# A convolution by short transforms: how the kernel weights are loaded and spread at the start

## The chip, the cores and the metric

The kernel runs on one core of a Trainium2 chip. The core has five engines that run side by side and meet only at semaphores: TensorE (matrix products into PSUM, an accumulator memory of eight banks), VectorE, ScalarE and GpSimd (elementwise work; only the first two of these read PSUM here), and SyncE, which issues transfers between the chip's main memory and the on-chip memory SBUF (128 partitions). The metric is the device time of one execution in microseconds; lower is better. In the profile TensorE appears as PE (the products) and PEld (the loading of the stationary operand), VectorE as DVE, ScalarE as ACT, GpSimd as POOL, SyncE's transfer issues as SPq.

## The reference

An image of 224 x 224 pixels with 96 channels is convolved, around its edges, with a 7 x 7 kernel from 96 to 96 channels, by way of the Fourier transform:

```python
B, H, W, C = x.shape          # 1, 224, 224, 96
K = w.shape[0]                # 7
wp = pad(w, ((0, H - K), (0, W - K), (0, 0), (0, 0)))
Xf = rfft2(x.astype(float32), axes=(1, 2))
Wf = rfft2(wp.astype(float32), axes=(0, 1))
Yf = einsum('bhwi,hwio->bhwo', Xf, Wf)
y = irfft2(Yf, s=(H, W), axes=(1, 2)).astype(bfloat16)
```

Inputs and outputs are bfloat16. Since the kernel is only 7 rows and columns, the same result can be had by short transforms over blocks.

## The kernel before, in words

Rows are cut into eight blocks of 28 (`NJ`, `B`), each transformed over 34 rows (`L`), which gives 17 frequencies (`NS`). Columns are not transformed; along them the seven taps are applied directly, with three products saved by sums and differences of taps and of even and odd columns (`TAPS`, ten tap combinations per frequency, `NTAP`). The image is cut along its width into seven tiles of 32 columns. For each tile three things are done:

- The forward transform ("A" jobs): pixels in SBUF are the stationary operand, the transform matrix `Fm` the moving one; the result goes from a PSUM bank to a buffer `xf` (two of them, alternating by tile) by an evacuation on VectorE or ScalarE. `evac` chooses the engine by an estimated load of each; `BIAS` is the estimate's starting value for VectorE.
- 17 rounds of products ("b rounds"), one for each frequency: `xf` or sums and differences of it (`J`, made by VectorE in `jit`, for three frequencies at a time) times the transformed weights `WF`, then sums on VectorE, ScalarE and GpSimd into `yf`, which SyncE stores to a scratch in main memory.
- The inverse transform ("C" jobs) with the matrix `G`, from the scratch to the output.

Tiles 0 and 1 run interleaved, tile 1 four rounds behind (`LAG`). Each engine runs its instructions in the order of the program text, and so does SyncE with the transfers. Within a round there are two places, `mid` and `end`, at which other jobs are filled in. A list of jobs is given by `add(a, b, jobs)` a stretch of such places: place k = 2r is the middle of round r, 2r + 1 its end, and `pace` hands the jobs out evenly from place a up to place b − 1.

The weights are transformed on the chip as well ("prep" jobs). The raw weights lie in the tile `wq` (`wqx`), which also holds the table `Em` of coefficients behind the weights' columns, and zeros behind that (`zw`). Partitions 2k and 2k + 1 both belong to the kernel position k of 49. Before the change both hold the weights of position k, the odd one shifted by 48 output channels (`C2`), so that one matmul yields the output channels o and o + 48. The stationary operand of such a matmul is `wqx[0:98, o : o + 127*96 + 1 : 96]`: one output channel of every input channel, thus a read with a step of 96 elements. The moving operand is `Em`, with a column for each frequency part and tap and each of the two halves. Frequencies go in groups (`PGRP`): group 0 is frequencies 0 and 1, the others three each. For group 0 all three parts (real, imaginary and their difference) come from the matmul: five slots of ten taps, twice, 100 columns, 48 matmuls, four to a bank, twelve evacuations. For later groups two parts come from matmuls of 120 columns, and the third is a subtraction on VectorE (`diff`), once for each frequency.

The start of the program (lines 160 to 282 and 683 to 705), which all engines run through in this order:

- SyncE: four transfers for the left edge pixels of tile 0 (`xh_bufs`), two for its first half of rows (`load_x(0, 0)`), two for the weights (line 188: 96 partitions, then the last two), two for tile 0's second half (`load_x(0, 1)`).
- TensorE: 17 warming matmuls on a tile of zeros (`warm`), the edge pixels, the first half's pixels (`fj[p][0]`, ten banks), 27 more warming matmuls, the 48 weight matmuls of group 0, then the second half's pixels for the first eight frequencies (`fj[0][1]`).
- VectorE: small tables, `Fm`, `Em` (lines 280 to 282), then evacuations, then the planes of the first three frequencies (`jit(0, 0)`).
- ScalarE: a first Sin that loads its function table, the zeros `zw` (line 222), the Sin of the tables, evacuations.
- GpSimd: index tables, masks, and the matrix `G`.

Tile 1's pixels are loaded with a wait on the first of the second half's evacuations (lines 696 to 698). In the rounds, the weight jobs of group g are spread from the group before it (line 730), tile 1's pixel jobs start at round 1 (lines 748 to 755), and the rest of tile 0's second half (`fj[1][1]`) is spread over places 0 to 3 (line 747).

Of the kernel before, what the change touches and what calls it, by code (L numbers as in the profile page):

```python
# [9 lines left out]
F32 = mybir.dt.float32  # L10
ALU = mybir.AluOpType
# [14 lines left out]
NB = 8  # L26
POS = TW + HALO
NTAP = 10
TAPS = ((7, 8, 9, 6), (0, 2, 4, 6), (1, 3, 5))
NSLOT = 2 + 3 * (NS - 1)  # L30
# [11 lines left out]
MERGE = ()  # L42
NP2 = 0
WARM = 12
BIAS = 2000.0


def slot(s, part):
    return part if s == 0 else 2 + 3 * (s - 1) + part
# [3 lines left out]
def kernel(  # L53
# [7 lines left out]
    _, H, W, C = x.shape  # L61
# [8 lines left out]
    C2 = C // 2  # L70
# [37 lines left out]
    def bank():  # L108
        return pools["psb"].tile([128, 512], F32, name="pb")
# [5 lines left out]
    def apart(key, zone, r):  # L115
        for z, q in parts.setdefault(key, []):
            if z != zone and q.engine != r.ins.engine:
                tc.declare_no_dep(r.ins, q, reason="disjoint parts of one tile")
        parts[key].append((zone, r.ins))
        return r  # L120
# [17 lines left out]
    def dma(out_ap, in_ap):  # L138
        return DE.dma_start(out=out_ap, in_=in_ap)
# [19 lines left out]
    stmp = stmp_cm.__enter__()  # L159
    wqx = wtmp.tile([128, C - 1 + 127 * C + 1], BF16, name="wq")  # L160
    wq = wqx[0:PW2]
    WC = C * C - C2
    Em = wqx[0:PW2, WC:WC + 2 * NSLOT * NTAP].rearrange("p (h a t) -> p h a t", h=2, a=NSLOT)
    XHW = PAD * C + 32
    late = WF[0:R, NSLOT - 8:NSLOT].rearrange("p a t o -> p (a t o)")
    x0_bufs = [late[:, i * (XW + 32):(i + 1) * (XW + 32)] for i in range(2)]
# [14 lines left out]
    def load_x(t, jg):  # L181
        return load_rows(xbuf(t, jg), jg, t * 2 * TW, 2 * TW)
# [2 lines left out]
    for jg in range(2):  # L185
        load_rows(xh_bufs[jg], jg, W - PAD, PAD)
    load_x(0, 0)
    for k, n in ((0, PW - 1), (PW - 1, 1)):
        dma(wqx[2 * k:2 * (k + n), 0:WC], bass.AP(wsrc.tensor, wsrc.offset + k * C * C, [[C * C, n], [C2, 2], [1, WC]]))
    load_x(0, 1)  # L190

    wu = cpool.tile([128, 128], BF16, name="wu")
    wur = wu[:].unsqueeze(1).to_broadcast([128, 4, 128])
    VE.memset(wu[:], 0.0)

    def warm(n):
        pwu = bank()
        for _ in range(n):
            TE.matmul(pwu[:].rearrange("p (a b) -> p a b", a=4), lhsT=wu[:, 0:128], rhs=wur, start=True, stop=True)
    warm(8)  # L200
    warm(9)

    ntmp = [0]

# [13 lines left out]
    VE.memset(pi_t[:], math.pi)  # L218
    dmy = ftile([128, 1])
    SE.activation(out=dmy[:], in_=pi_t[:], func=ACTF.Sin, bias=0.0, scale=0.0)  # L220
    zw = wqx[0:PW2, WC + 2 * NSLOT * NTAP:]
    SE.copy(out=zw, in_=wu[0:PW2, 0:1].to_broadcast(list(zw.shape)))

    nrj = ftile([R, JG]); pw_i = ftile([R, 1]); aa = ftile([R, NS, 2]); phf = ftile([R, NS, 2]); phe = ftile([R, NS, 2])
    twc = ftile([PW2, KT]); mf = ftile([R, JG, NS * 2])
# [51 lines left out]
    VE.tensor_single_scalar(out=pv[:, :, 0], in_=qe[:, 1:, 0], scalar=-2.0, op=ALU.mult)  # L277
    VE.tensor_tensor(out=pv[:, :, 1], in0=qe[:, 1:, 1], in1=qe[:, 1:, 0], op=ALU.subtract)
    VE.tensor_tensor(out=pv[:, :, 2], in0=pv[:, :, 0], in1=pv[:, :, 1], op=ALU.subtract)
    for k0, k1 in ((0, slot(PGRP[0][1], 0)), (slot(PGRP[0][1], 0), NSLOT)):  # L280
        VE.tensor_tensor(out=Em[:, :, k0:k1], in0=pe3[:, k0:k1].unsqueeze(1).unsqueeze(3).to_broadcast([PW2, 2, k1 - k0, NTAP]),
                         in1=mk2[:].unsqueeze(2).to_broadcast([PW2, 2, k1 - k0, NTAP]), op=ALU.mult)

    def build_g(nj):
        PG = nj * FR

        def floor_g(out_ap, in_ap, d):
            GE.tensor_scalar(out=out_ap, in0=in_ap, scalar1=1.0 / d, scalar2=-(d - 1) / (2.0 * d), op0=ALU.mult, op1=ALU.add)
            GE.tensor_single_scalar(out=out_ap, in_=out_ap, scalar=MAGIC, op=ALU.add)
            GE.tensor_single_scalar(out=out_ap, in_=out_ap, scalar=MAGIC, op=ALU.subtract)  # L290

        def mod_g(out_ap, in_ap, fl_ap, d):
            floor_g(fl_ap, in_ap, d)
            GE.tensor_single_scalar(out=out_ap, in_=fl_ap, scalar=-float(d), op=ALU.mult)
            GE.tensor_tensor(out=out_ap, in0=out_ap, in1=in_ap, op=ALU.add)
        p = ftile([PG, 1]); sp = ftile([PG, 1]); rm = ftile([PG, 1]); jp = ftile([PG, 1]); rr = ftile([PG, 1]); z = ftile([PG, 1])
        iota(p[:], [[0, 1]], cm=1)
        mod_g(rm[:], p[:], jp[:], FR)
        mod_g(rr[:], rm[:], sp[:], 2)
        GE.tensor_single_scalar(out=z[:], in_=sp[:], scalar=0.0, op=ALU.is_equal)  # L300
        zr = ftile([PG, 1]); ag = ftile([PG, 1]); pg = ftile([PG, 1]); amp = ftile([PG, 1]); pgt = ftile([PG, 1])
        GE.tensor_tensor(out=zr[:], in0=z[:], in1=rr[:], op=ALU.mult)
        GE.tensor_scalar(out=ag[:], in0=zr[:], scalar1=17.0, scalar2=sp[:, 0:1], op0=ALU.mult, op1=ALU.add)
        GE.tensor_single_scalar(out=ag[:], in_=ag[:], scalar=2.0, op=ALU.mult)
        GE.tensor_tensor(out=pgt[:], in0=rr[:], in1=zr[:], op=ALU.subtract)
        GE.tensor_scalar(out=pg[:], in0=pgt[:], scalar1=17.0, scalar2=17.0, op0=ALU.mult, op1=ALU.add)
        GE.tensor_scalar(out=amp[:], in0=z[:], scalar1=-1.0 / L, scalar2=2.0 / L, op0=ALU.mult, op1=ALU.add)
        nm = ftile([PG, nj, B]); jc = ftile([PG, nj, B]); msk = ftile([PG, nj, B]); fl = ftile([PG, nj, B]); th = ftile([PG, nj, B])
        iota(nm[:], [[0, nj], [1, B]], base=PAD)
        iota(jc[:], [[1, nj], [0, B]])  # L310
        GE.tensor_scalar(out=msk[:], in0=jc[:], scalar1=jp[:, 0:1], scalar2=amp[:, 0:1], op0=ALU.is_equal, op1=ALU.mult)
        GE.tensor_scalar(out=nm[:], in0=nm[:], scalar1=ag[:, 0:1], scalar2=pg[:, 0:1], op0=ALU.mult, op1=ALU.add)
        mod_g(th[:], nm[:], fl[:], Q)

        def fin():
            SE.activation(out=th[:], in_=th[:], func=ACTF.Sin, bias=pi_t[0:PG, :], scale=-2.0 * math.pi / Q)
            GE.tensor_tensor(out=G.rearrange("p (j m) -> p j m", j=nj), in0=th[:], in1=msk[:], op=ALU.mult)
        return fin

    g_fin = build_g(3)  # L320

    def prep_jobs(gi):
        s0, s1 = PGRP[gi]
# [364 lines left out]
    for p in range(2):  # L688
        for f in fj[p][0]:
            f()  # L690
    for _ in range(3):
        warm(9)
    for f in prep_jobs(0)[0]:
        f()
    last = [f() for f in fj[0][1]]
    for jg in range(2):
        for d in load_x(1, jg):
            tc.add_manual_dep(d.ins, last[0].ins.name, SYNC, reason="second tile's pixels later")
    for f in jit(0, 0):
        f()  # L700
    g_fin()
    stmp_cm.__exit__(None, None, None)
    yf_pool = ctx.enter_context(tc.tile_pool(name="yf", bufs=YBUF))
# [21 lines left out]
    def add(a, b, jobs):  # L725
        qs.append([a, b, jobs, len(jobs)])

    for gi in range(1, len(PGRP)):
        pj, dj = prep_jobs(gi)
        add(2 * PGRP[gi - 1][0], 2 * PGRP[gi - 1][1] - 1, pj)  # L730
        for i, f in enumerate(dj):
            k = 2 * (PGRP[gi][0] + i) - 2
            add(k, k + 1, [f])
    for t in range(2):
        scr_tiles[t] = dr_pool.tile([TW, NJ, NS, 4 * C], BF16, name="scr")
# [9 lines left out]
    for r in range(NS + LAG):  # L745
        if r == 0:
            add(0, 4, fj[1][1])
        for p in range(2):
            if r == (1, 3)[p]:
                new_xf(1, SH2[1][p], SH2[1][p + 1])  # L750
                fj = f_jobs(1, p)
                if p == 1:
                    for jg in range(2):
                        fj[jg][-1] = then_load(fj[jg][-1], 2, jg)
                add(2 * r + 1, 2 * r + (5, 8)[p], fj[0] + fj[1])
        for p in range(3):
            if r == (9, 14, 17)[p]:
                new_xf(2, SH2[2][p], SH2[2][p + 1])
                fj = f_jobs(2, p)
                if p == 2:  # L760
                    for jg in range(2):
                        fj[jg][-1] = then_load(fj[jg][-1], 3, jg)
                add(2 * r, 2 * r + (8, 7, 5)[p], fj[0] + fj[1])
        if r == PGRP[-2][1] + 1:
            assert not any(q[2] for q in qs[:4 * len(PGRP) - 8])
            wtmp_cm.__exit__(None, None, None)
            t_pool = ctx.enter_context(tc.tile_pool(name="tt", bufs=NTT, side="right"))
            t2_pool = ctx.enter_context(tc.tile_pool(name="tt2", bufs=1, side="right"))
            yo_pool = ctx.enter_context(tc.tile_pool(name="yo", bufs=2, side="right"))
            g_pool = ctx.enter_context(tc.tile_pool(name="gp", bufs=1, side="right"))  # L770
            GA = g_pool.tile([KA, 4 * B], BF16, name="GA")
            GB = g_pool.tile([128, 2, 4 * B], BF16, name="GB")
            GE.memset(GA[:], 0.0)
            GE.memset(GB[:], 0.0)
        if r == NS + 3:
            queue_c(0)
        for t in range(2):
# [123 lines left out]
```

## Time and profile before

| | us |
|---|---|
| median of nine runs (lowest, highest) | 277.96 (275.99, 279.67) |
| the profiled execution | 277.17 |
| its span, first to last instruction | 275.4 |

Busy time by engine, as a share of the span: PE 260.3 us (95%), PEld 238.6 us (87%), DVE 227.8 us (83%), ACT 196.5 us (71%), POOL 101.2 us (37%). An engine that is busy for a large share is not thereby the bound in every stage; stages have to be read one at a time.

Some points of the start, from the timeline (us from the span's start):

| engine | what | start, duration |
|---|---|---|
| SyncE | issues of the edge pixels and the first half of tile 0 (6) | 0.81, 2.27 |
| SyncE | issues of the weights (2) | 3.12, 1.19 |
| SyncE | issues of the second half of tile 0 (2) | 4.35, 0.70 |
| SyncE | issues of tile 1's pixels (4) | 22.65, 1.42 |
| VectorE | memset of the zero tile, 64 words | 0.89, 0.11 |
| ScalarE | zeros `zw`, 98 x 2120 | 2.20, 1.94 |
| ScalarE | Sin of the tables | 4.05, 0.43 |
| VectorE | `Em`, two instructions (0.26 and 1.10) | 6.33, 1.39 |
| VectorE | first six evacuations | 7.64, 3.15 |
| VectorE | planes of the first three frequencies (3) | 23.68 to 25.64 |

"Idle before" in square brackets at the end of a timeline row is the time in which the engine stood still just before it, with what ended the wait.

### The profile page before, as it was taken

Reading aid. Unit: us, or ns where it says so; the run is one execution under the profiler, and the core shown is the slowest. Engines: PE = TensorE matmul, PEld = TensorE weight load, DVE = VectorE, ACT = ScalarE, POOL = GpSimd, SP = SyncE. Lnnn points to the kernel's source line nnn. Section 1 sums busy time; section 2 is a strip of 40 time slices with the busy share of each in tenths; the row PEclk is TensorE's granted clock in tenths of the full one; section 3 lists DMA queues with packets and bytes.
Section 4 is the critical chain, followed back from the end, with each engine's and each line's share of the span. In section 5 each row is a group of like instructions: output and inputs, shape, how many; then the busy total and the mean of one; then the engine's idle time right before and its main releaser. Section 6 shows DMA issues by size and latency. Waiting matters only on the chain.

```text
span 275.4 us, 12056 instructions
## 1 busy us (share of the span) xinstructions
PE 260.3 (95%) x5088; PEld 238.6 (87%) x5088; DVE 227.8 (83%) x469; ACT 196.5 (71%) x475; POOL 101.2 (37%) x152
## 2 busy tenths in 40 slices
PE   8879999989998999999999999999999999999971
PEld 3559998989998998999999999999999999999750
DVE  5539999999999889878977897788988889899932
ACT  5429997768873656997988879888897874653532
POOL 7720033444545552332343224222422333644100
PEclk9989999999999999999999999999999999999999
DMA  6945113511021198996959487977949833988765
GB/s 177 223 114 160 56 48 108 153 43 57 36 88 46 48 272 169 264 291 168 318 162 263 120 244 220 221 198 214 277 141 187 268 122 119 200 214 233 198 182 177
DMA packets 46211, 46.79 MB, mean 170 GB/s; under 512 B 35274, under 2 KB 37846, under 8 KB 46058
## 3 DMA queue, kind: packets, MB, share of 16 engines
q1 hardware_dynamic: 45692, 44.34, 59.2%
q0 software_dynamic: 464, 1.67, 1.7%
q8 instruction: 40, 0.66, 1.0%
q14 instruction: 15, 0.12, 0.2%
HBM read 24.65 MB, written 21.33 MB: 167 GB/s over the span
## 4 chain that ended last, share of the span: by engine, by line
PE 57%; DVE 16%; DMA 10%; issue 6%; ACT 4%; POOL 3%; SPq 1%; ACTq 0%; DVEq 0%; POOLq 0%
PE pb L87 57%; DVE J L87 7%; DMA wq<-in_w_dram 5%; DVE WF L87 3%; POOL yf L87 3%; DVE v L87 3%; DMA xf<-scrl 3%; DMA scrl<-yf 2%; ACT xf L87 2%; DVE u L87 2%; ACT WF L87 2%; SPq L87 1%; DVE yf L87 1%; DVE yo L87 0%; DVE xf L87 0%
## 5 line engine op out<-in xcount | busy, mean ns | idle before, releaser
L87 PE MATMUL pb<-WF,J 96*128 96x96 bf16 x2898 | 167.7, 206 | 1.0 <-DVE J L87 0.3
L87 PEld LDWEIGHTS <-J 96*128 96x128 bf16 x2898 | 141.5, 98 | 10.8 <-DVE J L87 1.6
L87 POOL TENSOR_TENSOR yf<-v,u 128x384 bf16<-128x384 f32 x85 | 84.2, 1006 | 142.8 <-issue 90.2
L87 ACT CAST xf<-pb 96x408 bf16<-96x408 f32 (+5 forms) x142 | 66.9, 491 | 7.3 <-PE pb L87 5.4
L87 PE MATMUL pb<-WF,xf 96*128 96x96 bf16 x952 | 61.0, 206 | 2.9 <-DVE WF L87 2.2
L87 DVE TENSOR_TENSOR J<-xf 96x1824 bf16<-96x1824 bf16 (+1 forms) x84 | 60.3, 757 | 0.1
L87 PEld LDWEIGHTS <-xf 96*128 96x128 bf16 x952 | 47.4, 98 | 3.8 <-issue 3.1
L87 PE MATMUL pb<-Fm,xn 118*128 118x136 bf16 (+4 forms) x576 | 44.6, 203 | 0.3 <-issue 0.3
L87 ACT CAST WF<-pb 96x480 bf16<-96x480 f32 (+1 forms) x60 | 30.0, 560 | 8.3 <-PE pb L87 8.1
L87 PE MATMUL pb<-tt,Gm 102*84 102x384 bf16 (+1 forms) x132 | 33.6, 326 | 0.0
L87 PEld LDWEIGHTS <-xn 118*128 118x128 bf16 x576 | 29.2, 98 | 0.1
L87 ACT CAST yo<-pb 84x384 bf16<-84x384 f32 (+1 forms) x61 | 26.3, 479 | 4.1 <-PE pb L87 3.2
L87 ACT CAST J<-pb 84x384 bf16<-84x384 f32 (+1 forms) x62 | 26.8, 482 | 2.7 <-PE pb L87 2.7
L87 DVE TENSOR_TENSOR J<-J 96x912 bf16<-96x912 bf16 (+1 forms) x42 | 25.0, 594 | 0.0
L87 PE MATMUL pb<-wq 98*128 98x120 bf16 (+1 forms) x288 | 22.9, 234 | 1.8 <-DMA wq<-in_w_dram 1.8
L87 PEld LDWEIGHTS <-wq 98*128 98x128 bf16 x288 | 20.6, 151 | 2.3 <-issue 2.3
L87 PE MATMUL pb<-wu 128*128 128x512 bf16 (+3 forms) x70 | 18.2, 387 | 1.1 <-DVE ct L87 1.1
L87 DVE TENSOR_TENSOR yf<-v,u 128x384 bf16<-128x384 f32 x27 | 15.6, 579 | 0.9
L87 DVE TENSOR_TENSOR WF<-WF 96x960 bf16<-96x960 bf16 x15 | 15.8, 1056 | 0.2
L87 PEld LDWEIGHTS <-wu 128*128 128x128 bf16 (+3 forms) x70 | 7.7, 113 | 8.0 <-issue 2.2
L87 DVE CAST WF<-pb 96x400 bf16<-96x400 f32 (+1 forms) x12 | 7.2, 607 | 8.2 <-PE pb L87 7.9
L87 PEld LDWEIGHTS <-Gm 102*84 102x84 bf16 (+1 forms) x132 | 11.5, 117 | 1.7 <-issue 0.6
(394 smaller groups left out, 236.8 us busy)
## 6 DMA issues: line engine op xcount, KB each, us to landing
scr<-yf SPq DMA_DIRECT2D x30, 288.0 KB
xn<-in_x_dram SPq DMA_DIRECT2D x12, 672.0 KB
tt<-scr SPq DMA_DIRECT2D x24, 336.0 KB
out_dram<-yo SPq DMA_DIRECT2D x12, 252.0 KB
out_dram<-J SPq DMA_DIRECT2D x12, 252.0 KB
tt<-scr SPq DMA_DIRECT2D x6, 288.0 KB
wq<-in_w_dram SPq DMA_DIRECT2D x1, 1719.0 KB
scrl<-yf POOLq DMA_DIRECT2D x5, 288.0 KB, 5.0
```

The costliest lines, as they stand in the source:

```text
L87: r = fn(*a, **k)
```

## The change

One copy of the weights is loaded first: position k's weights on partition 2k alone, in three pieces of columns (0, 3072, 6144, 9216) for positions 0 to 47, and the last position's row by itself (`load_wl`), which is issued ahead. The odd partitions below it are zeroed beforehand, with all rows 0 to 95: the first third of the columns by VectorE's memset, the other two by ScalarE, as 32-bit words. The table `Em` moves 48 columns back, as a whole weight row now lies before it; the zeros behind it are written by VectorE instead of ScalarE. `beside` tells the dependency tracker that these writes do not depend on the weight transfers.

Group 0 is now made by `first_prep`: 96 matmuls, one for each output channel, with the 50 columns of `Em`'s first half, over 97 partitions; eight to a bank, twelve evacuations of 400 columns as before. The first six banks stand ahead of the second half's pixels `fj[0][1]`, three behind them, then the planes `jit(0, 0)`, then the last three. The second copy of the weights, on the odd partitions, is issued behind all that (`load_w(1, ...)`, `load_wl(1, ...)`); the later groups use both copies with 120 columns as before.

Tile 1's pixels are issued right behind tile 0's, without the former wait. The weight jobs of group 1 now all stand at place 3, the end of round 1, with their first difference; tile 1's first pixel jobs start in round 0 and run over places 0 to 2. Warming matmuls are 10 + 11 and twice 5, instead of 8 + 9 and three times 9. `BIAS` becomes 0.

```diff
-BIAS = 2000.0
+BIAS = 0.0
...
-    WC = C * C - C2
-    Em = wqx[0:PW2, WC:WC + 2 * NSLOT * NTAP].rearrange("p (h a t) -> p h a t", h=2, a=NSLOT)
+    WA = C * C
+    WC = WA - C2
+    WZ = WA // 3
+    Em = wqx[0:PW2, WA:WA + 2 * NSLOT * NTAP].rearrange("p (h a t) -> p h a t", h=2, a=NSLOT)
...
-    for k, n in ((0, PW - 1), (PW - 1, 1)):
-        dma(wqx[2 * k:2 * (k + n), 0:WC], bass.AP(wsrc.tensor, wsrc.offset + k * C * C, [[C * C, n], [C2, 2], [1, WC]]))
-    load_x(0, 1)
+    wld = []
+
+    def load_w(h, cuts):
+        for a, b in zip(cuts[:-1], cuts[1:]):
+            wld.append(dma(wqx[h:2 * PW - 3 + h:2, a:b], wsrc[0:PW - 1, h * C2 + a:h * C2 + b]))
+
+    def load_wl(h, n):
+        wld.append(dma(wqx[2 * PW - 2 + h:2 * PW - 1 + h, 0:n], wsrc[PW - 1:PW, h * C2:h * C2 + n]))
+    load_wl(0, WA)
...
     VE.memset(wu[:], 0.0)
+    VE.memset(wqx[0:PW2 - 2, 0:WZ], 0.0)
...
-    warm(8)
-    warm(9)
+    warm(10)
+    warm(11)
...
-    zw = wqx[0:PW2, WC + 2 * NSLOT * NTAP:]
-    SE.copy(out=zw, in_=wu[0:PW2, 0:1].to_broadcast(list(zw.shape)))
+    zw = wqx[0:PW2, WA + 2 * NSLOT * NTAP:]
+
+    def zero(ap):
+        o = ap.bitcast(F32)
+        SE.copy(out=o, in_=wu[0:ap.shape[0], 0:2].bitcast(F32).to_broadcast(list(o.shape)))
+    for i in range(1, 3):
+        zero(wqx[0:PW2 - 2, i * WZ:(i + 1) * WZ])
+    load_w(0, (0, WZ, 2 * WZ, WA))
+    load_x(0, 1)
+    for jg in range(2):
+        load_x(1, jg)
...
+    def beside(r):
+        for d in wld:
+            tc.declare_no_dep(r.ins, d.ins, reason="columns behind the weights")
     for k0, k1 in ((0, slot(PGRP[0][1], 0)), (slot(PGRP[0][1], 0), NSLOT)):
...
+    beside(VE.memset(zw, 0.0))
...
+    def first_prep():
+        n = slot(PGRP[0][1], 0)
+        q = n * NTAP
+        wv = WF[0:C, 0:n].rearrange("i a t o -> i (a t) o")
+
+        def mk_(o0):
+            def f():
+                pw = bank()
+                pv_ = pw[:, 0:NB * q].rearrange("p (k q) -> p k q", q=q)
+                for k in range(NB):
+                    o = o0 + k
+                    TE.matmul(pv_[:, k], lhsT=wqx[0:PW2 - 1, o:o + 127 * C + 1:C], rhs=Em[0:PW2 - 1, 0, 0:n].rearrange("p a t -> p (a t)"), start=True, stop=True)
+                apart(("W", 0), o0, evac(wv[..., o0:o0 + NB], pv_[0:C].rearrange("i k q -> i q k"), NB * q))
+            return f
+        return [mk_(o0) for o0 in range(0, C, NB)]
...
-    for _ in range(3):
-        warm(9)
-    for f in prep_jobs(0)[0]:
+    for _ in range(2):
+        warm(5)
+    pj = first_prep()
+    for f in pj[:6]:
         f()
-    last = [f() for f in fj[0][1]]
-    for jg in range(2):
-        for d in load_x(1, jg):
-            tc.add_manual_dep(d.ins, last[0].ins.name, SYNC, reason="second tile's pixels later")
+    for f in fj[0][1]:
+        f()
+    for f in pj[6:9]:
+        f()
     for f in jit(0, 0):
         f()
+    for f in pj[9:]:
+        f()
+    load_w(1, (0, WC))
+    load_wl(1, WC)
     g_fin()
...
-        add(2 * PGRP[gi - 1][0], 2 * PGRP[gi - 1][1] - 1, pj)
+        add(*((3, 4) if gi == 1 else (2 * PGRP[gi - 1][0], 2 * PGRP[gi - 1][1] - 1)), pj)
         for i, f in enumerate(dj):
-            k = 2 * (PGRP[gi][0] + i) - 2
+            k = 2 * (PGRP[gi][0] + i) - (1 if gi == 1 and i == 0 else 2)
             add(k, k + 1, [f])
...
-            if r == (1, 3)[p]:
+            if r == (0, 3)[p]:
...
-                add(2 * r + 1, 2 * r + (5, 8)[p], fj[0] + fj[1])
+                add(2 * r + p, 2 * r + (3, 8)[p], fj[0] + fj[1])
```

More of the change, by code (lines that the diff above doesn't have):

```diff
@@ L279 @@
     VE.tensor_tensor(out=pv[:, :, 2], in0=pv[:, :, 0], in1=pv[:, :, 1], op=ALU.subtract)
+    def beside(r):
+        for d in wld:
+            tc.declare_no_dep(r.ins, d.ins, reason="columns behind the weights")
     for k0, k1 in ((0, slot(PGRP[0][1], 0)), (slot(PGRP[0][1], 0), NSLOT)):
-        VE.tensor_tensor(out=Em[:, :, k0:k1], in0=pe3[:, k0:k1].unsqueeze(1).unsqueeze(3).to_broadcast([PW2, 2, k1 - k0, NTAP]),
-                         in1=mk2[:].unsqueeze(2).to_broadcast([PW2, 2, k1 - k0, NTAP]), op=ALU.mult)
+        beside(VE.tensor_tensor(out=Em[:, :, k0:k1], in0=pe3[:, k0:k1].unsqueeze(1).unsqueeze(3).to_broadcast([PW2, 2, k1 - k0, NTAP]),
+                         in1=mk2[:].unsqueeze(2).to_broadcast([PW2, 2, k1 - k0, NTAP]), op=ALU.mult))
+    beside(VE.memset(zw, 0.0))
     def build_g(nj):
@@ L764 @@
         if r == PGRP[-2][1] + 1:
-            assert not any(q[2] for q in qs[:4 * len(PGRP) - 8])
+            assert not any(q[2] for q in qs if q[1] <= 2 * r)
             wtmp_cm.__exit__(None, None, None)
```

## The prediction, made before the changed kernel ran

> **What bounds the kernel now.** I read the page first, for where TensorE is not busy. Its 40 slices are 6.9 us each.
>
> ```profile
> PE   8879999989998999999999999999999999999971
> PEclk9989999999999999999999999999999999999999
> ```
>
> TensorE is full nearly everywhere; the third slice (13.8 to 20.7 us) is the weak one, and its clock drops there too. Nothing behind it changes except by a shift, so the question is when the first product of tile 0 can start, and how the rounds after it fare. The chain of waits, asked for the first 64 us, names what sets that start:
>
> ```profile
> 3.87 13.76 DMA wq<-in_w_dram
> ...
> 17.77 3.79 PE pb L87 x44
> 21.58 0.49 ACT WF L87
> 22.07 1.05 ACT xf L87 x2
> ...
> 23.16 2.78 PE pb L87 x54
> ...
> 30.20 0.66 DVE WF L87
> ```
>
> The weight transfer ends the wait at 17.77; from there it is TensorE, then evacuations on ScalarE, and round 0 starts at 23.16. The TensorE timeline shows what lies around that wait, with how many matmuls and how long:
>
> ```profile
> 7.96 2.13 PE L87 MATMUL pb<-Fm,WF 118*128 118x64 bf16 x64 [0.72 <-DMA WF<-in_x_dram]
> 9.93 6.00 PE L87 MATMUL pb<-wu 128*128 128x512 bf16 x27
> 17.77 4.00 PE L87 MATMUL pb<-wq 98*128 98x100 bf16 x48 [1.84 <-DMA wq<-in_w_dram]
> 21.61 1.10 PE L87 MATMUL pb<-Fm,WF 118*128 118x64 bf16 x32
> 23.16 0.52 PE L87 MATMUL pb<-WF,xf 96*128 96x96 bf16 x8 [0.46 <-ACT xf L87]
> 23.52 1.16 PE L87 MATMUL pb<-wq 98*128 98x120 bf16 x16
> 24.51 0.56 PE L87 MATMUL pb<-Fm,WF 118*128 118x72 bf16 x12
> 30.33 0.33 PE L87 MATMUL pb<-WF,xf 96*128 96x96 bf16 x4
> 30.90 0.33 PE L87 MATMUL pb<-WF,xf 96*128 96x96 bf16 x4 [0.24 <-DVE WF L87]
> ```
>
> From 9.93 to 15.93 TensorE only warms itself (27 matmuls on zeros), then idles 1.84 us: 7.8 us are to be won, no more. Round 2 waits at 30.9 for a weight difference. The table of single microseconds gives the price of the idle time and of a full clock (the last three figures of a row are the granted clock, the DMA share and GB/s):
>
> ```profile
> 16.00:17.00 1.00, 0.00 (x0) 0.00 (x0) 0.00 (x0) 0.00 (x0) 0.21 (x1) 1.00 0.68 160
> 18.00:19.00 1.00, 1.00 (x15) 1.00 (x14) 0.66 (x2) 0.42 (x1) 0.00 (x0) 0.52 0.08 31
> ```
>
> **The parts and their costs.**
>
> *Transfers.* Adding up that table's GB/s, 967 KB have moved by 6.0 us; the halos and the first pixels are 997 KB and are used at 7.96, so use follows the last byte by about 1.9 us. Traffic runs at 275 to 307 GB/s in 4 to 8 us and near 180 in 13 to 15, when only the long weight rows and the second half of the pixels remain. Before, 98 rows of 18.3 KB (1.80 MB) are ahead of the first weight matmul; after, 49 rows (0.90 MB), in three column pieces plus one row. Each piece has to wait for its zeroing. ScalarE's zeroing copy took 1.94 us for 2120 columns, 0.92 ns each, so two copies of 1536 words take 1.41 us each. They start after the pi tile, which now stands behind VectorE's new memset (1.3 us, below): about 2.75, so they end at 5.6. The pieces are issued from there to about 6.9 (0.35 us each, as SyncE's rows show), their bytes flow from about 7 and last 3.0 to 4.4 us at 300 to 200 GB/s, and with 1.9 us behind them the weights are usable at 12 to 13.4. The remaining pixels of tile 0 (0.72 MB) come 2.5 to 3.6 us later, at 14.5 to 17, those of tile 1 (1.45 MB) 5 to 7 us after that, at about 20 to 23: they are queued behind the pieces on SyncE, which stands still for the zeroing, where tile 0's were issued at 4.35 before.
>
> *VectorE ahead of that.* The memset of 1536 words: 64 words took 0.11 us and one word 0.06, so 0.8 ns a word, 1.3 us. The trace has no larger one on this engine; the slower bound is the 0.92 ns of the ScalarE copy, 1.45 us. [...] Everything on VectorE moves back, the Sin on ScalarE waits until 5.6 behind the zeroing (4.05 before), the table Em ends at about 8.6 (7.72 before; its 0.72 us wait for GpSimd is used up), and the tail zeroing that moves to VectorE (1036 words) adds 0.9. Its first evacuation starts at 9.6 instead of 7.64. Queued behind that are the evacuations of tile 0's halo; eight banks rotate, so the sixth pixel bank waits for the second halo's evacuation (to 10.1), the tenth for a bank that VectorE frees at 11.2. TensorE finishes these 64 matmuls at 11.35 rather than 9.93; two warm-ups of five (0.22 us each, 6.00/27) take it to 13.5. So TensorE itself, not the transfer, sets the start: 13.5 instead of 17.77, **−4.3 us**. Bounds: 12.1 (no delay by banks) to 14.4.
>
> *96 matmuls for 48.* The nearest row is the 120-column one on the same strided weights at full clock: 16 from 23.52 to 24.51, 62 ns each. Its weight load has a median of 147 ns, against 98 for dense pixels, whose 64-column matmuls run at 31 ns; so the strided load sets the pace and 50 columns don't shorten it. 96 x 62 ns is 5.95 us, against 3.84 before (48 from 17.77 to 21.61, 80 ns, at the halved clock): **+2.1 us**. From below, 96 x 31 ns is 3.0 us, −0.9; from above, at 80 ns, 7.7 us, +3.8. I take 62 because operand and stride are the same. The clock should stay full, as no idle time near 1.84 us is left in front.
>
> [...]
>
> *Rest of the head.* The 32 pixel matmuls of the second half move between the weight matmuls: 1.05 us as before, if their pixels are in at 16.5 (estimate 14.5 to 17). Twelve evacuations stay, of 400 columns each (0.49 and 0.64 us), hidden under 0.5 us of matmuls per bank on two engines. The last one costs what 23.16 − 22.7 costs now. Round 0 starts at 23.16 − 4.3 + 2.1 = **21.0**.
>
> *Rounds 0 and 1.* The 48 group-1 weight matmuls leave rounds 0 and 1 as filler and stand in one block at the end of round 1, so that the second copy may arrive; tile 1's first pixel jobs (64 matmuls) fill instead. Work is equal, only order changes. TensorE has 55 products at 43 ns, 32 + 64 pixel matmuls at 32: 5.5 us, so the block is due at 26.5. SyncE issues the second copy when the last first-group matmul is through, 20.5, behind the empty queue of tile 1's pixels; 1.1 us to first bytes (issue 0.81, traffic near 1.9), 0.9 MB at the 276 to 281 GB/s seen at 26 to 28 us is 3.3 us, 1.9 to use: 26.8. **+0.3 us**. What waits behind the issue on SyncE are only stores of round 2 and later. After the block, twelve evacuations (0.49 to 0.64 us) must end and one difference (0.65) run before round 2's third part; spread jobs left 0.24 us of that, the block leaves about 0.6 + 0.65 − 0.36 (eight products in between): 0.9, so **+0.7**. Bounds 0 and 1.3.
>
> *VectorE's planes for round 0* (2.0 us at 23.68) now run during the head, where it was idle; from 23 to 43 us VectorE and ScalarE are near full, and TensorE's waits there sum to 0.24 + 0.30 + 0.24 and some 0.15. I take **−0.6**, between 0 and −0.9. The changed starting value of the evacuation balance moves some two evacuations from ScalarE to VectorE, whose planes are done: 0, bounds ±0.5 (half of 1 us).
>
> Sum: −4.3 + 2.1 + 0.3 + 0.7 − 0.6 = **−1.8 us**. Against the profiled execution's own 277.17 that is 275.4; the median shown, 277.96, is 0.8 above it, so 276.2 as the median. The terms' bounds put this case at 275.0 to 277.3.
>
> **Rivals.** *More gain.* VectorE's delay doesn't reach TensorE (12.1) and the loads are nearer 50 ns than 62 (−1.1): −1.4 and −1.1 on top, less what the transfer at 12 to 13 gives back (0.7): −3.6, 274.4. For it: the dense loads take 31 ns. Against: the same operand at 62.
>
> *The second copy is late* (slower). One place: the block at 26.5. At the 180 GB/s that the weight rows ran at in 13 to 15 us, 0.9 MB is 5.0 us, use at 28.5, an idle time of 2.0 us: 1.7 more than summed. That is as long as the 1.84 us after which the clock halved; then the 48 matmuls of 120 columns go from 62 to 100 ns (100 columns took 83): +1.8. Sum +1.7, 279.6. It decides from a landing near 28.5. For it: half the partitions are written, as before each row is long. Against: an otherwise empty queue.
>
> *The pieces don't go early*, so the change doesn't do what it says: they write every second row of a tile zeroed in full rows. If each piece waits for the one before it as well, each takes 1.1 + 1.0 + 1.9 = 4 us from 5.6, the weights come at 17.6, the doubled matmuls are pure loss: +2.1 + 0.7 − 0.6 − 0.1 = +2.1, 280.0. The diff exempts only the table from such waits; nothing shown excludes the rest.
>
> *Nothing left*: block and banks at their upper bounds, −1.8 + 0.9 + 0.6 = −0.3, 277.6.
>
> **Numbers.** Forecast 0.45 (of it 0.33 beyond half a per cent, 0.12 within), more gain 0.20, late copy 0.14, pieces waiting 0.09 (0.07 slower), nothing left 0.12. Half a per cent (1.4 us) is about what a measurement can tell from no change. Faster 0.53, same 0.26, slower 0.21. Range 273.8 to 279.4; the forecast's own 275.0 to 277.3.
>
> **What would show it.** First weight matmul near 13.5 with at most a short wait for a transfer; 96 in about 6 us; round 0 at 21; the clock full from 13 to 27; the block near 26.5 with a wait under 0.5 us; round 2's wait for a difference near 0.9. I am wrong if the first weight matmul waits past 15, if the loads are spaced 100 ns, or if the block waits 2 us.

## The result: slower by one per cent

| | before | changed |
|---|---|---|
| median | 277.02 us (51 runs) | 279.69 us (16 runs) |
| ratio to before, 95% interval | | 1.0102 [1.0073, 1.0130] |
| span of the profiled execution | 275.4 us | 278.3 us |
| mean granted clock in it | 0.991 | 0.982 |

The forecast was 276.2 us with a range to 279.4; the change costs about 2.7 us instead of gaining 1.8. The ratio leaves out the three slowest of the change's 16 executions (282.8 to 283.2 us, some 22 us at half clock each). The page of the changed kernel, TensorE's busy time and granted clock in 40 slices of 7.0 us:

```profile
PE   8999798998998999999999999999999999999963
PEclk9965999999999999999999999999999999999999
```

The third slice is full now (9, before 7); the fifth, 28 to 35 us, is the weak one (7). And the clock row has two bad slices (6 and 5) where before it had one (8). The TensorE timeline of the changed kernel has the steps that the prediction counted (start, duration, operation, number of instructions, idle time before it and what ended it; "..." stands for rows left out):

```profile
13.33 3.07 PE L87 MATMUL pb<-wq 97*128 97x50 bf16 x48
16.24 1.87 PE L87 MATMUL pb<-Fm,WF 118*128 118x64 bf16 x32
17.92 3.01 PE L87 MATMUL pb<-wq 97*128 97x50 bf16 x48
21.50 0.80 PE L87 MATMUL pb<-WF,xf 96*128 96x96 bf16 x8 [0.58 <-ACT WF L87]
...
28.88 3.17 PE L87 MATMUL pb<-wq 98*128 98x120 bf16 x48
31.88 0.33 PE L87 MATMUL pb<-Fm,WF 118*128 118x72 bf16 x5
33.65 0.33 PE L87 MATMUL pb<-WF,J 96*128 96x96 bf16 x4 [1.44 <-ACT WF L87]
33.82 0.33 PE L87 MATMUL pb<-WF,xf 96*128 96x96 bf16 x4
34.78 0.33 PE L87 MATMUL pb<-WF,xf 96*128 96x96 bf16 x4 [0.63 <-DVE WF L87]
...
45.40 0.33 PE L87 MATMUL pb<-WF,xf 96*128 96x96 bf16 x4 [1.28 <-DVE WF L87]
```

The first weight matmul comes at 13.33 (4.4 us earlier) with no wait for a transfer, and round 0 starts at 21.50 instead of 23.16. So at 21.5 us the change is ahead by 1.66 us. The products at 45.40 (round 5) stand at 42.61 in the trace of before, with as many weight and pixel matmuls done by then:

```profile
41.85 0.34 PE L87 MATMUL pb<-WF,J 96*128 96x96 bf16 x4 [0.30 <-DVE WF L87]
42.03 0.33 PE L87 MATMUL pb<-WF,xf 96*128 96x96 bf16 x4
42.61 0.33 PE L87 MATMUL pb<-WF,xf 96*128 96x96 bf16 x4 [0.24 <-DVE WF L87]
```

There the change is 2.8 us behind, which is nearly the whole difference of the two spans (2.9). Between these two points 4.45 us were given back. The table of stretches shows the first half of it. Its columns are the stretch, its length, the busy time of PE, PEld, DVE, ACT and POOL (with the number of instructions), then the granted clock, the DMA share and GB/s:

```profile
13.00:16.40 3.40, 3.40 (x55) 3.20 (x54) 1.60 (x3) 0.98 (x2) 2.83 (x7) 0.98 1.03 269
16.40:19.80 3.40, 3.40 (x65) 3.40 (x63) 2.25 (x5) 2.32 (x5) 0.00 (x0) 0.50 0.71 184
19.80:23.20 3.40, 2.82 (x46) 2.73 (x45) 2.17 (x4) 3.08 (x9) 0.36 (x1) 0.50 0.35 81
23.20:26.60 3.40, 3.40 (x62) 3.40 (x60) 2.03 (x4) 1.80 (x4) 0.00 (x0) 0.51 0.67 183
```

From 16.4 to about 26.4 TensorE has half its clock, although the row ahead of the fall (13.0 to 16.4) shows it busy without a gap. The 32 pixel matmuls take 1.68 us (16.24 to 17.92) instead of the 1.05 of the forecast, and rounds 0 and 1 up to the block take 7.4 us (21.50 to 28.88). The second half is the row of idle times ahead of round 2 (1.44 + 0.63 us; 0.24 before) and of round 5 (1.28; 0.30 + 0.24 before). What stands ahead of the first of them, from ScalarE's and VectorE's timelines:

```profile
29.35 4.25 ACT L87 CAST WF<-pb 96x480 bf16<-96x480 f32 x9 [0.28 <-PE pb L87]
```

```profile
29.91 1.40 DVE L87 TENSOR_TENSOR J<-xf 96x1824 bf16<-96x1824 bf16 x2
31.23 0.62 DVE L87 TENSOR_TENSOR J<-J 96x912 bf16<-96x912 bf16 x1
31.78 1.77 DVE L87 CAST WF<-pb 96x480 bf16<-96x480 f32 x3
34.08 0.66 DVE L87 TENSOR_TENSOR WF<-WF 96x960 bf16<-96x960 bf16 x1 [0.53 <-ACT xf L87]
```

VectorE is making the planes of rounds 3 to 5 when the block's banks fill, so nine of the twelve evacuations fall to ScalarE in a row; the difference that round 2 needs can only follow at 34.08.

### The profile page after: what moved, and what is told of

Same layout as the page of the kernel before. It is cut to its first block, busy times and chain, and to the rows that moved or that the text cites. A ratio compares the mean times of both kernels' runs of the same rounds, so it can differ in the third digit from the quotient of the medians.

```text
span 278.3 us, 12139 instructions
## 1 busy us (share of the span) xinstructions
PE 262.7 (94%) x5123; PEld 242.4 (87%) x5123; DVE 230.1 (83%) x470; ACT 198.2 (71%) x477; POOL 100.7 (36%) x152
## 3 DMA queue, kind: packets, MB, share of 16 engines
q0 software_dynamic: 464, 1.67, 1.8%
## 4 chain that ended last, share of the span: by engine, by line
PE 58%; DVE 20%; DMA 7%; issue 6%; ACT 5%; POOL 2%; SPq 0%; DVEq 0%
PE pb L87 58%; DVE J L87 7%; DMA tt<-scr 5%; DVE WF L87 4%; DVE v L87 4%; ACT WF L87 3%; POOL yf L87 2%; DVE u L87 2%; ACT xf L87 1%; DMA xf<-scrl 1%; DVE yf L87 1%; DVE yo L87 1%; SPq L87 0%; DVE tt L87 0%; ACT yo L87 0%
## 5 line engine op out<-in xcount | busy, mean ns | idle before, releaser
L87 PE MATMUL pb<-Fm,xn 118*128 118x136 bf16 (+4 forms) x576 | 45.3, 206 | 0.0
L87 PEld LDWEIGHTS <-xn 118*128 118x128 bf16 x576 | 30.1, 100 | 0.1
L87 ACT CAST J<-pb 84x384 bf16<-84x384 f32 (+1 forms) x61 | 26.4, 481 | 2.4 <-PE pb L87 2.4
L87 PE MATMUL pb<-wq 98*128 98x120 bf16 (+1 forms) x336 | 24.5, 226 | 0.0
L87 PEld LDWEIGHTS <-wq 98*128 98x128 bf16 (+1 forms) x336 | 22.5, 152 | 0.2
L87 PE MATMUL pb<-wu 128*128 128x512 bf16 (+3 forms) x57 | 16.2, 406 | 1.1 <-DVE wu L87 1.1
L87 DVE TENSOR_TENSOR WF<-WF 96x960 bf16<-96x960 bf16 x15 | 16.5, 1101 | 0.5 <-ACT xf L87 0.5
L87 PEld LDWEIGHTS <-wu 128*128 128x128 bf16 (+3 forms) x57 | 6.7, 120 | 7.1 <-issue 3.3
L87 DVE CAST xf<-pb 96x512 bf16<-96x512 f32 (+4 forms) x17 | 9.6, 590 | 3.0 <-PE pb L87 3.0
```

Source lines behind the costliest of these rows:

```text
L87: r = fn(*a, **k)
```

## The experiments

Two suspects follow: the clock (A) and the block (C). The profile of one execution is not enough for the clock, because it varies from execution to execution of one kernel (a mean of 0.961 to 0.991 over the 16 of the change). Each timed run lists its mean granted clock, and in the traces of before and of the change every recorded value of the clock is 1 or 0.5, so 2 x (1 − clock) x span is its time at half clock. Over the executions that the comparisons use, before has 3.8 us of it on average and the change 9.3. Time and half-clock time go together: a straight line through 82 executions of before gives 275.3 us and 0.34 us for each microsecond at half clock (correlation 0.74), through 13 of the change 277.1 us and 0.24 (0.80). By that there is also something that is not the clock; but no execution of the change has less than 5 us at half clock, so 277.1 is a line drawn beyond its points. Not all of this time lies at the start: in six of the fourteen traces kept some 3 us of it lie within the last 11 us of the kernel. All ratios below are to the kernel before on the same chip.

**100 columns instead of 50 in the first 96 matmuls.** The added columns are the table's next ones, and their results are not read. Four matmuls fill a bank, so there are 24 evacuations of half the size; the lists of banks ahead of and behind the pixels are doubled to match.

```diff
-                for k in range(NB):
+                for k in range(4):
...
-                    TE.matmul(pv_[:, k], ..., rhs=Em[0:PW2 - 1, 0, 0:n].rearrange("p a t -> p (a t)"), ...)
+                    TE.matmul(pv_[:, k], ..., rhs=Em[0:PW2 - 1, 0].rearrange("p a t -> p (a t)")[:, 0:100], ...)
...
-        return [mk_(o0) for o0 in range(0, C, NB)]
+        return [mk_(o0) for o0 in range(0, C, 4)]
```

> The changed kernel, but each of the 96 first-group matmuls streams 100 columns (both halves of the table; the second half meets zeroed rows and is not read), four to a bank, 24 evacuations of half the size. Theory A (the clock halves because 50 streamed columns in about 149 cycles at full clock leave the array two thirds empty for a whole window): granted clock 1.0 from 13 to 27 us, spacing still about 62 ns, the second-half pixels 1.05 us instead of 1.7, round 0's first products start near 20.9 instead of 21.5, the group-1 block starts near 26 instead of 28.9, and the time falls by 2 to 2.7 us, to about that of the kernel before. Rival B (the clock falls for another reason: the head's bank waits or the transfers): clock 0.5 from 16.4 to 26.4 as in the changed kernel, time unchanged within 0.5 us.

(Where the expectation says that the added columns are those of the second half: they are the next 50 of the first half, which belong to later frequencies; the streaming is the same. Its 149 cycles are an estimate that counts a streamed column as a cycle: in the trace of before the warming matmuls in a row, of 512 columns each, start 215 to 216 ns apart, 2.4 columns a nanosecond, and 62 ns at that rate are about 147 columns. Of these 50 are 34%, and the 64 and 80 of the later expectations 44% and 54%.) Its timeline and two of its stretches:

```profile
13.50 3.15 PE L87 MATMUL pb<-wq 97*128 97x100 bf16 x48
...
21.00 0.50 PE L87 MATMUL pb<-WF,xf 96*128 96x96 bf16 x8 [0.41 <-ACT WF L87]
...
27.10 3.14 PE L87 MATMUL pb<-wq 98*128 98x120 bf16 x48 [0.84 <-DMA wq<-in_w_dram]
...
31.89 0.33 PE L87 MATMUL pb<-WF,J 96*128 96x96 bf16 x4 [1.48 <-ACT WF L87]
```

```profile
16.40:19.80 3.40, 3.40 (x74) 3.40 (x74) 2.88 (x7) 2.71 (x9) 0.00 (x0) 1.00 0.68 181
...
33.40:36.80 3.40, 3.40 (x45) 3.40 (x43) 2.04 (x4) 2.35 (x6) 0.97 (x1) 0.54 0.02 5
```

The clock in the head is full in this execution, and the matmuls are as quick with twice the columns, as theory A says. But the time did not fall: 1.0103 [1.0046, 1.0161]. The block is reached earlier, waits 0.84 us for the second copy, leaves the same 1.48 us behind it, and now the clock falls there, for 3.4 us.

**64 columns.** The same with eight to a bank, `[:, 0:64]`.

> The changed kernel with 64 streamed columns in the 96 matmuls instead of 50 (14 further columns of the table, not read afterwards), eight to a bank, twelve evacuations as before; 64 of about 149 cycles is 43%. Theory A with a limit below 0.43: clock full, gain as with 100 columns, 2 to 2.7 us. Theory A with a limit above 0.43: clock as in the changed kernel, time the same. Rival B: the same as the changed kernel. Alone it tells only where the limit lies, beside the run with 100 columns.

The profiled execution has full clock from 13 to 30 us too, and again a fall behind the block; 1.0109 [1.0042, 1.0177]. In time it tells no more than the run with 100.

**The block on two places.**

```diff
-        add(*((3, 4) if gi == 1 else ...
+        add(*((2, 4) if gi == 1 else ...
```

> The changed kernel with the twelve group-1 weight jobs at places 2 and 3 (six in the middle of round 1, six at its end) instead of all at place 3. Theory C (the block's twelve evacuations, nine of which fell to ScalarE in a row, plus the difference cost round 2 some 2.1 us of TensorE idle, 1.44 + 0.63, against 0.24 before): the idle falls below 1.2 us and the time by 0.7 to 1.3 us, the clock unchanged. Rival D (VectorE and ScalarE are simply full there, the idle only marks where their backlog shows): the idle appears in another place and the time stays within 0.4 us.

Neither came. It is slower still, 1.0169 [1.0100, 1.0239]: the first six jobs wait 2.39 us for the second copy at 26.87, and 1.53 + 0.37 us stay ahead of round 2. A shorter block is no cure while its input lands at 27. This execution is also a warning: with the same 50 columns its clock stayed full until 32.9 us. The fall in the head happens in some executions, not in all.

**The balance's start value.**

```diff
-BIAS = 0.0
+BIAS = 2000.0
```

> The changed kernel with the starting value of the evacuation balance back at 2000. If my price of 0 with bounds of 0.5 us holds: within 0.5 us of the changed kernel. If the new start value loads VectorE so that the weight differences come late (the 1.28 us wait at 45.4, against 0.24 and 0.30 before): that wait falls below 0.6 and the time by 0.7 us or more.

1.0093 [1.0049, 1.0137] against the change's 1.0102: no difference, as priced. The wait ahead of round 5 did fall, to 0.26 us in the profiled execution, but TensorE came late there: its clock was at half from 17.2 to 27.5 and again from 34.3 to 41.1 us. With 100 columns and a shorter fall behind the block the same wait was 0.51 us, so it tells little about the balance.

**Clock and both its sources.** 100 columns, and seven warming matmuls where TensorE idled behind the block.

```diff
         if r == 0:
             add(0, 4, fj[1][1])
+            add(3, 4, [lambda: warm(7)])
```

> The changed kernel with 100 streamed columns in the 96 matmuls and seven warming matmuls between the group-1 block and round 2, where TensorE idled 1.4 to 2.1 us. Theory A (the time lost is mostly the halved clock, and it has two sources, the short matmuls of the head and the idle time behind the block): time at half clock under 3 us in most executions (from the mean granted clock: 2 x (1 - clock) x span), median 276 to 277, level with the kernel before. Rival E (the structure itself costs some 1.8 us, as the executions at nearly full clock suggest): the clock is full as well, but the median stays 1.5 us or more above that of the kernel before at like clock, near 277.5.

The page's clock row, and the timeline at the block:

```profile
PEclk9999999999999999999999999999999999999999
```

```profile
26.89 3.12 PE L87 MATMUL pb<-wq 98*128 98x120 bf16 x48 [1.03 <-DVE v L87]
30.01 1.68 PE L87 MATMUL pb<-wu 128*128 128x512 bf16 x7
...
32.34 0.33 PE L87 MATMUL pb<-WF,xf 96*128 96x96 bf16 x4 [0.19 <-DVE WF L87]
...
42.93 0.33 PE L87 MATMUL pb<-WF,xf 96*128 96x96 bf16 x4 [1.25 <-DVE WF L87]
```

Mean time at half clock is 2.1 us, and the ratio falls from 1.0102 to 1.0039 [1.0010, 1.0067], a median of 277.29. The clock is not all of the loss: with a fuller clock than before has, the kernel is still 0.9 us slower by the medians, 1.1 by the ratio. The block still stops TensorE for 1.0 us ahead of it, the warming only takes the place of the idle time behind it, and 1.25 us stay ahead of round 5.

**Only the warming behind the block** (50 columns).

> The changed kernel with only the seven warming matmuls behind the block, 50 streamed columns as in the change. Beside the two runs with 100 columns it separates the two sources of the halved clock: theory A has the head's low clock stay (0.5 from about 16.4) and the one from 30 us on go, with a mean time at half clock of 6 to 9 us against 11.7 of the changed kernel's executions, and the time 0.5 to 1.2 us lower. If the short matmuls alone are the source, time and clock stay as in the changed kernel.

Mean time at half clock 6.2 us, ratio 1.0049 [1.0007, 1.0090]. The profiled execution has the fall in the head, from 17.0 to 27.3, and none behind the block, which the runs with 100 and 64 columns, on two places and with the start value of 2000 all have. That fits two sources, as theory A has it, but the change's own trace has no fall behind the block either. Over executions, the warming takes the mean from 6.4 us (four) to 2.1 (twelve) with 100 columns.

The twelve executions of this one kernel also give the price of the fall, as they form two groups: six have 11.1 to 12.2 us at half clock and a mean of 279.5 us, six have at most 2.8 us and a mean of 276.4. The halved clock is worth 3.1 us here, the larger part of the change's loss. Without it the kernel is 0.7 us slower than the ten executions of before beside it that have as little half clock (275.7). The run with 100 columns and the same warming has none of twelve above 5.5 us at half clock; its seven executions at full clock take 277.2 us, 0.8 more than the six here. Which of its differences costs that, 24 evacuations or the longer wait ahead of the block, was not separated.

**The kernel before with nine more warming matmuls.**

```diff
-    for _ in range(3):
+    for _ in range(4):
         warm(9)
```

> The kernel before with nine more warming matmuls ahead of its weight matmuls (36 instead of 27), which fill its 1.84 us of waiting for the weights. Theory A: the 3.4 us at half clock from 18.0 go in most executions, the 48 weight matmuls come at 62 ns instead of 80 (0.9 us), the time falls by 0.7 to 1.3 us. Rival (the idle time does not cause the fall of the clock): clock and time as before, or slower by up to 0.3 us where the warming outlasts the wait.

Time at half clock fell from 3.5 us in the executions of before beside it to 2.3 on average, the 48 matmuls came at full clock in the profiled execution and round 0 at 22.59 instead of 23.16. Yet the ratio is 1.0001 [0.9978, 1.0025]: the expected 0.7 us or more did not show. At the 0.34 us of the line above, 1.1 us less at half clock is only some 0.4 us, which this interval can hide; and ten of the 28 executions of before beside it have at most 2.8 us at half clock, so no whole fall of 3.4 us that the warming could remove.

**The kernel before with the block.** Its own head; only the placing of group 1 from the change, with its first difference.

> The kernel before with only the placing of the group-1 weight jobs from the change: all twelve at place 3 with the first difference. Nothing fills places 0 to 2 in their stead. Theory C (the block costs its evacuation tail): TensorE idles 1.4 to 2.1 us ahead of round 2's products instead of 0.24, and the time rises by 1.2 to 2 us, by up to 3 where the clock halves behind it. Rival D: the idle time only moves, the time stays within 0.5 us of the kernel before.

```profile
27.62 3.16 PE L87 MATMUL pb<-wq 98*128 98x120 bf16 x48
...
33.02 0.34 PE L87 MATMUL pb<-WF,J 96*128 96x96 bf16 x4 [1.16 <-DVE WF L87]
...
33.78 0.48 PE L87 MATMUL pb<-WF,xf 96*128 96x96 bf16 x4 [0.15 <-DVE WF L87]
```

1.0131 [1.0085, 1.0178], 3.2 us between the medians, from six executions: in the kernel before, the block costs as much as the whole change does. It is not quite the block alone, as here nothing fills places 0 to 2 (a wait of 0.84 us for the planes adds to it), and the clock falls behind it (9.1 us at half clock on average). Rival D, by which the idle time only moves, is out.

**Three frequencies in the first group, no block.** If the two causes are right, they can both be removed: the strided loads set the pace from 50 to 120 columns (61 to 62 ns a matmul), so a third frequency is free, group 1 is needed a round later, and 80 columns keep the array fuller.

```diff
-PGRP = ((0, 2), (2, 5), (5, 8), (8, 11), (11, 14), (14, 17))
+PGRP = ((0, 3), (3, 5), (5, 8), (8, 11), (11, 14), (14, 17))
...
-        return [mk_(o0) for o0 in range(0, C, NB)]
+        return [mk_(o0) for o0 in range(0, C, 6)]
...
-        add(*((3, 4) if gi == 1 else ...
+        add(*((3, 6) if gi == 1 else ...
```

There are 16 banks now: eight ahead of the pixels, four behind them, then the planes, then four.

> The changed kernel with the first three frequencies, not two, by the 96 matmuls: 80 columns each (54% of 149 cycles), six to a bank, 16 evacuations of 480 columns; the next group has two frequencies, its twelve jobs (80 columns, 320 to evacuate) spread over places 3 to 5 instead of standing in a block. Theory F (the earlier start is worth what was forecast, about 2 us, and was given back by the block and by the clock): the 96 matmuls still take 6 us, since the strided loads set their pace, round 0 starts at 20.5 to 21, the clock is full from 13 to 30, no wait above 0.7 us ahead of rounds 2 and 3, median 1 to 2.5 us below the kernel before (274 to 275.5). Rival E (something else of the new order costs about 2 us): the waits are gone and the clock is full, yet the time is not below that of the kernel before.

```profile
12.65 3.07 PE L87 MATMUL pb<-wq 97*128 97x80 bf16 x48
...
20.52 0.50 PE L87 MATMUL pb<-WF,xf 96*128 96x96 bf16 x8 [0.95 <-ACT WF L87]
...
26.04 1.17 PE L87 MATMUL pb<-wq 98*128 98x80 bf16 x16 [0.27 <-DMA wq<-in_w_dram]
...
31.30 0.33 PE L87 MATMUL pb<-WF,J 96*128 96x96 bf16 x4 [0.59 <-ACT WF L87]
```

275.74 us, ratio 0.9961 [0.9927, 0.9995]: clearly faster than the change, and by little, if at all, faster than before. The interval just leaves out 1; those of three kernels like it, below, do not. The 48 matmuls of 80 columns take the 3.07 us that 48 of 50 took. The gain is under the 1 to 2.5 us expected: a wait of 0.95 us stands ahead of round 0 now (four evacuations in a row on ScalarE while VectorE makes planes), 0.59 + 0.19 ahead of round 3, and the time at half clock is 6.4 us on average.

The same with the balance at 2000:

> The same with the starting value of the evacuation balance at 2000. If the balance matters only by which engine takes the first evacuations of the rounds: within 0.5 us of the run with three frequencies. If VectorE's differences come late because of the lower value, 0.7 us or more faster.

275.67 us, 0.9984 [0.9948, 1.0020]; the two are alike. In its profiled execution the clock fell in the head once, from 21.1 to 24.5, in spite of the 80 columns, behind the 0.94 us that TensorE waits ahead of round 0.

**Filling those waits, and moving the planes.** Four warming matmuls ahead of round 0 and group 1 at places 3 and 4; then also the planes behind the last evacuations. Both have the balance at 2000.

```diff
     for f in pj[12:]:
         f()
+    warm(4)
...
-        add(*((3, 6) if gi == 1 else ...
+        add(*((3, 5) if gi == 1 else ...
```

> The kernel with three first frequencies and the balance at 2000, with four warming matmuls in the 0.94 us that TensorE waits ahead of round 0, and the next group's jobs at places 3 and 4, so that its difference at place 5 has one place of cover. Theory A and F: the 0.51 + 0.27 us ahead of round 3 shrink below 0.3 us, the time at half clock falls from 5 to 6 us on average to under 4, and the median falls by 0.5 to 1 us, to 274.7 to 275.2, clear of the kernel before. Rival: the clock's falls come from elsewhere, time at half clock and median as with three frequencies (275.7).

> The same with VectorE's planes for round 0 behind the last four evacuations instead of ahead of them. If the wait ahead of round 0 comes from four evacuations in a row on ScalarE: it falls from 0.94 us to about 0.5, but the planes end some 1 us later and round 0's second products wait for them; sum within 0.4 us of the run beside it.

0.9972 [0.9938, 1.0005] and 0.9979 [0.9942, 1.0015]. The mean time at half clock went to 3.8 and 3.5 us, as expected, but the wait moved on to the second copy (0.47 and 0.66 us) and the one ahead of round 3 stayed (0.61 and 0.55). No gain over the plain three frequencies is shown, where 0.5 to 1 us was expected. The second copy, on which group 1 waits until 26.0 to 27.0 in three of the four traces with three frequencies, seems to bound this order of work; no run moved its landing.

**Emptiness or idle time: a count over all traces.** Whether a sparse stream of matmuls or idle time as such lowers the clock can be read from the fourteen kept traces. In each of them the clock falls and returns only at steps of 3.41 us. So each trace can be divided at these steps, from 8 us on, and the moving columns of the matmuls that start in each window added up, as far as the window and the next lie inside the span. Warming matmuls in a row stream 512 columns in 0.216 us, about 8100 in a window. Some windows:

| kernel | window from, us | columns | TensorE idle in it, us | clock in the next window |
|---|---|---|---|---|
| before | 14.6 | 3060 | 1.85 | half |
| changed | 12.9 | 3552 | 0 | half |
| changed | 29.9 | 4080 | 1.14 | full |
| 100 columns | 13.2 | 5632 | 0 | full |
| 100 columns | 30.3 | 3144 | 1.67 | half |
| 64 columns | 15.4 | 4544 | 0 | full |
| block on two places | 12.4 | 3886 | 0 | full |
| block on two places | 15.9 | 3998 | 0 | full |
| three frequencies, balance 2000 | 17.6 | 3576 | 0.94 | half |

In the changed kernel's window from 12.9 these are two warming matmuls, 48 of 50 columns and two of 64. Of 1047 windows at full clock 17 were followed by half clock, and all 17 have fewer than 3960 columns. Only six others have so few; of the 1024 with 3990 or more none was followed by a fall, though some have up to 1.5 us of idle time. Three of the 17 have no idle time at all: they hold the matmuls of 50 columns. So it is how little is streamed in a window that lowers the clock, about half of the full stream being the limit in these traces, and idle time counts as one way to stream little. It also explains the chance: the steps lie elsewhere in each execution, and with 50 columns the windows of the head come out close to the limit, at 3360 to 3998 columns.

## Why the prediction was wrong, step by step

*Transfers and VectorE's delay: right.* The memset took 1.34 us (1.3 in the sum), the table Em ended at 8.63 (forecast 8.6), the first evacuation began at 9.64 (9.6), and TensorE was ready at 13.33 (13.5). An agreement within 0.2 us is partly luck: in the ten other traces with this head the first weight matmul comes between 12.52 and 13.81. The rival in which the pieces wait for one another is out: they were issued between 3.1 and 7.5 us, and no matmul waited for them.

*96 matmuls for 48: right.* 48 took 2.91 us (13.33 to 16.24), 61 ns each against the 62 of the sum. They kept that pace at half clock, and with 64, 80 or 100 columns, where dense operands with 64 columns went at 31 ns; so the strided load of the stationary operand is taken to be the limit. At full clock one such load takes 160 ns in this trace (median of the first 48; 98 ns for the dense pixels of 8.1 to 10.5 us), and the matmuls start 61 ns apart, far from the 100 ns at which the prediction would have been wrong.

*"The clock should stay full, as no idle time near 1.84 us is left in front": this step failed.* I took idle time for what lowers the clock. A row of matmuls that stream 50 columns every 61 ns, 21 ns of work at the 2.4 columns a nanosecond of the warming matmuls (512 in 0.216 us), leaves the array two thirds empty, and the profile calls that busy. In the trace of before the clock halved behind the 1.84 us of idle time, for 3.41 us (18.0 to 21.4); in that of the change it halved for 10.24 us, three such steps (16.3 to 26.5), and this fall came without an idle gap. Against the sum it cost 0.6 us at the pixels and 1.9 us in rounds 0 and 1 (7.4 us for 5.5; in the run with three frequencies, with full clock there, they take 5.3, from 20.52 to 25.8). More columns and warming behind the block bring the clock back, and 1.9 us of the mean with it (279.3 to 277.4); the two groups of executions of the run with the warming alone are 3.1 us apart. That the emptiness of a window is the measure is shown by the count over the fourteen traces, down to a few windows near the limit; the timing of the steps decides whether one execution falls.

*The block, +0.7, was mis-sized.* The wait ahead of round 2 was 2.07 us, where the sum had 0.9. I shared twelve evacuations evenly; VectorE was at its planes, and nine went to ScalarE. In the kernel before, the block costs 3.2 us, together with the fall of the clock behind it and a wait for the planes.

*The second copy, +0.3: the landing right, the wait not.* In the change the block came late enough not to wait; with full clock (100 columns) it waited 0.84 us for a landing at 27.1 (forecast 26.8). The slower rival, a late second copy, was not the mechanism, though the clock that it used as a price was.

*VectorE's planes, −0.6: not seen.* The waits that they were to remove grew, to 1.28 us ahead of round 5; this is 0.7 us more than before. It stays at 1.25 us in both runs with warming behind the block, and is 0.26 to 0.99 where the clock fell behind the block and TensorE came late. So VectorE's work sets when round 5 begins; why it lags more than before stays open.

Sum of what was off, in the profiled executions: 0.5 (round 0 at 21.50 instead of 21.0, by the clock at the pixels) + 1.9 (the clock in rounds 0 and 1) − 0.3 (no wait for the second copy) + 1.2 (round 2: 2.07 us, not 0.9) + 1.3 (the planes: +0.7, not −0.6) = 4.6 us, which takes −1.8 to the +2.8 measured. One execution's clock is a draw. Over many, some 2 us of the 2.8 between the means of the change and of before come with the clock, and 0.7 to 1.1 remain without it, by the two runs with warming behind the block.

## What to carry to other kernels

A busy engine in the profile is not a busy array (here a window of 3.41 us with 48 of the 50-column matmuls had no idle time and streamed 3552 columns, of some 8100): before trading one matmul for two half as wide, compare the columns streamed in a few microseconds with what back-to-back matmuls would stream, and look at the granted clock behind it, in several executions. When work is gathered into a block so that a late transfer may arrive, price the tail of the block on the engine that will really empty it, together with what that engine has queued. And where the loading of the stationary operand sets the pace, wider products cost TensorE hardly any time (up to 100 columns here: 48 matmuls took 3.07 us with 50 columns, 3.15 with 100), so use the width for work that removes a later wait.

## What the runs showed of the hardware, unexpected

A stationary operand read with a step of 192 bytes set a pace of 61 to 62 ns a matmul, from 50 to 120 columns at full clock, and with 50 columns at half clock too; dense ones with 64 columns went at 31 ns in the trace of before. The clock halved, in the changed kernel at 16.3 us, behind a stretch in which TensorE had no gap at all, and in all fourteen traces only behind windows of 3.41 us with fewer than 3960 streamed columns, about half of the full stream. It came back after 14 of the 15 half-clock windows with 4050 columns or more, which is all that the halved clock lets through (before: 4100 columns from 18.0 to 21.4), and stayed low after nine of the twelve with fewer.
